# A state-space convolution with a gated feed-forward block: one set of tables for both channel halves, ungated loads, halved last tiles and a new task list

## The chip, the cores and the metric

One core of one Trainium2 chip runs the whole program. The metric is the device time of one execution in microseconds. A core has five engines with queues of their own: PE (TensorE, the matmuls), DVE (VectorE), ACT (ScalarE), POOL (GpSimd) and SP (SyncE, which here only issues DMAs); ACT also issues some DMAs. Sixteen DMA engines serve all of these queues.

## The reference, cut to what matters

```python
def _A_ref(u, A_re, A_im, B_re, B_im, C_re, C_im, log_dt, Dskip):   # u: (1, 2048, 512)
    dt = exp(log_dt)[:, None]
    logdA = dt * (A_re + 1j * A_im)                                  # (512, 128)
    K = einsum("dn,dnl,dn->dl", Cc, exp(logdA[:, :, None] * l), dt * Bc).real
    y = irfft(rfft(pad(u)) * rfft(pad(K)))[:L]                       # causal convolution, length 2048
    return y + u * Dskip

def _B_ref(x, w_gate, w_up, w_down):                                 # 512 -> 1792 -> 512
    return (silu(x @ w_gate) * (x @ w_up)) @ w_down

x = A_u
xn = layernorm(x)
s = _A_ref(xn, ...)
g = silu(_B_ref(xn, B_w_gate, B_w_up, B_w_down))
return x + s * g
```

Each of the 512 channels is convolved with its own kernel K of length 2048; the feed-forward block works on rows of 512.

## The kernel before, in words

**The work.** The feed-forward block is cut into 56 units (8 blocks of 256 rows, 7 chunks of the 1792 hidden columns). A unit has a gate half and an up half (`half_mm`, L699, 24 matmuls each, because every f16 operand is split into a high and a low part) and two groups of six down matmuls (`down`, L741). The weights are scaled and split first: `w_norm` (L604) sums squares, `norm_sum` (L614, L615) adds them over the partitions with a matmul on a tile of constants called `ones`, `w_scale_gu` (L635, L624, L637) makes the scale, `w_split` (L669, L670, L665 to L667) makes high and low parts. Rows of u are normalized by `ln_group` and `x_norm` (L503 to L531) and transposed (L540, copied by L546). A row tile ends with `z`, a PSUM bank that collects all down matmuls, and a SiLU of it on ACT (L748), called `zg`; ten of the sixteen `zg` tiles go out to DRAM (`zg_d`) and come back.

The convolution is a Fourier transform in two stages. `x_stage1` (L563) transforms u and stores it in `ax_d`; `kg_tables`, `kg_trig`, `kg_prod`, `kg_mm` (L1145) and `kg_s1` (L1178) build K and store its first stage in `ak_d`, channel half c = 0 ahead of c = 1. Stage two works on 8 groups n of frequencies for each channel half: `s2_load` loads `ak_d`, `ax_d` and a table `gj` of 320 KB; `s2_mm` and `s2_prod` (L1230, L1237) transform and multiply; `s2_inv` (L1277) transforms back two groups together and stores to `bs_d`, with SP issuing the stores (L1289). `final` loads `bs_d`, u again (L1309) and, for early rows, `zg_d`; does the last inverse matmuls (L1324), multiplies by `zg` on DVE (L1333), adds u on POOL (L1336) or for the last rows on DVE (L1338), and stores from ACT's queue (L1340). There are 14 tiles of two row tiles by half the channels, and the two last row tiles alone with all channels.

**The order.** All of this is a list of tasks. Each `add` names an engine, a duration and the buffers and keys that it reads and writes. A long string, `LIST`, gives the order in which tasks are written out; the queue of each engine runs in that order and waits by semaphores. A small model (`Plan.run`) runs through the same list to choose PSUM banks and places in an arena of 118 KB per partition, within `ROOM`, and `keep_warm` puts filler matmuls on `ones` (L1423) where the model sees PE idle. The model's numbers thus change banks, places and fillers, and nothing of what an instruction takes on the chip. DMAs of one queue are issued in order: one that waits holds those behind it.

**Gates.** In `s2_load` the three loads wait for everything stored under the keys `ax` and `ak0` or `ak1`. In `final` the loads of u and of `zg_d` carry `ready`, the key of all `bs_d` stores of the channel half, as the load of `bs_d` itself does.

Of the kernel before, what the change touches and what calls it, by code (L numbers as in the profile page):

```python
# [13 lines left out]
I32 = mybir.dt.int32  # L14
AF = mybir.ActivationFunctionType
ALU = mybir.AluOpType
# [31 lines left out]
    "#)#(#'#K#&#%#J#L#.#T#i#M#N#k###l#/#O#U#R#j#m#V#n#1#v#P#2#Q#S#D#Y#4#W#-#X#Z#5#+#w#o#x#y#q#,#p#r#*&+#8#z(*#s#t&.(+"  # L48
    "#]&/(,(.#}$&#7#[$'$(${(/$)#C#d#;#{#^&0#|$#(0#e(4#_#`&E#f%S&3$*#g&,#a$+#h#b#c(-#:$$(1$-#<&5$w&v(5$2&:&8$x(6$z$y$,"
    "#>$1$3$|$.(7&=#9%#$/(:(;$4$}#=&;#A(@&x$5$6$<%%%.$7&4$=$>(L$8(<%&(M&A$?$@$k$H$G$I(F(2#@(N$;%$(3&9#?$C&1&u#B$9(=&F"  # L50
    "%/(>%((H$D%2$J#0$K(?#6#3(G(I$:$A$S$R$T$N(O$L$B$t(A(R(S(B(J(K$E&6$F$O$](T$M(X(Z$q(P#E&J(C&@$%&?$Q(8(9(Q$0&y$P#u$U"
    "%)&B(_%T(a(D$V&>(U&C&k%+$^$_&}(V(W$Y(Y([$W%'%7(e(g(`$e(b$X%0$Z$[$b(](c&7(E(d(}$`%*(^)$(f(h(i$h$a$f$c%8%<(w$n$i$l"
    "%9$d$m(x(j(y(k$u(m%-%B%,%A%5(z)#({$j%C$r%P$o$s#$#I(l(n(q%D%:(r%Q%R(o)((|$g)=%6)>)?)))0)F%E$p%=$v)G%>%3%F%?(p)H&D"
    "&I&a)%%G%H&G&L%I%;&H(s&V&K%J&M%L)1)2%M)3):%K%@%4-F%1)I&N&O&Q&P)R)S&W)&)J%N&b-G-K);(t&<)<-L&T)T&2)U)'(u&X#G-M&l(v"
    "&c%O&Y%W&m)])^&w'#&R-H&n&p&o&[-I&q&d&f&i&e&])_&S-J-N)`&_-O&z&^&Z)b-R)*&`)K&s&t'$)i)j-P%V-Q-S&g&h&j-[-`-]&U-U-V-X"
    "-k)k)l)s)t-l)c)+-x-c-W-Y-T-d)@-^-_)B-b-a-y.5#H)a-e-g&-)d-f)A-t-v.6),-|.#&r-o-q.7-Z-h)--m-n-p.4)4)6-r%U-s).)/)L.8"
    ".9)C.:.;-u.$-i-j.%)5)7-z-{)w-}.&.(.')8)9.<-w)D.B)E.W.C.E.D.F)u.).*.+)N.I)V)M.?.A%Y)O.=.>.@.H)W)P)x%`)Q#F.,.e.J.K"
    ".M)e.G%]..)X.-./.L.N*$.X.Q.S.O.P%Z.R)Y)Z.T%[.0.1)m%a._.`%d.f)y'')n.b.3.U.2)z)f)[)o*%){)g%X%i'1.[.^.l.m)h*&.Y)p.a"
    "*'.o*()v.V**.c.|.Z)q%b.])|)r.i.k.n.p.g.h.}/#/$*..j%^/%%e*1)}/&/'/(*#%j.d.q.r%c.s*2//*3%k*)*:%n%f*/%g%s.t&{*0.v%_"
    "/).u*;*+*B*4*C.w%h.x.y.z.{/*/+%o%p*</,/./-*6*D*E/5%t/6/0%q/1/3*,/7%l*-/2/D*5*F*7/8/:/Q/9/>&|%m%r&)*G/</4*>/;/S%u"  # L60
    "*8/@*9%v*=*?/=';/?/E*L&'*M/F/H'%/G*@%w*H*A/R/j/I/k/l/M*N*P*I*J/J/O/K/L*K/i*O%y/N'&/A/B*Q*T*U*V*]/Z/]*X/T/V/X/Y'("
    "*R/[/m/n')/U'**S/W'</P/^*W/C/o/p'2/_*Y*Z'3'=/q*[*h%x/}'+/r/s/`*^'4'5/t/u*o/v*e'E'F'G/a*f*g*i',/c/d'T/e%z&#'6'/%{"
    "/b/f/h/g/y&$*j'9'7*_/{%|'-*k*l'.0U&%*a01/w/x0#&&%}&*/z'>*`*b'?0$'H'I*p0%02*c*q*d*m0&0>*n0+/|0:0<&(0V*w0(0?0X0W0'"
    "*x0Z+$0)+%0[0-*r030*0,'U050B0D0G0Y0^07040I0@0A0C'V0.+.0]'00806'J'M090;0E+/*s0_'@0F0`'N0H*t0/00':'K0=0J0a'S'Y'A'B"
    "+&+''C'D+0*u*v0b0K*y0L0n0c0d0e0g0h0i0k+1+60f*z1/0j0M'q0l0Q'L0p0O0o'Z'O0P0N1#*{0u0v0m+(0r0t0R0S0w0}100q0s*|+)1$+*"
    "0T0y*}+#++0x1G+21H1)1*'R'P1F1J+31K1L1,1I+7+81%1'0z+,+-+:1+1-+4+51315'W181:+911+;12141&1(0{0|'{1617+I19+>+<1M'Q1Q"
    "+=1T1U1O+?+@+A1N'81.'X'['g1[1W']1;1<1P1=+F+G1R'|'}+B+C1>1B1Z1V'^'_1]1^1S1x+D1X1@1_'r'h's'i1A+P1j+Q+X+Y1b1a+a+b't"
    "+E1?1C(#'`1c1e'j1E1w+J'k1k'a1s1d+L($1f+K+c1`24251Y1g+M1l'u1m1o'b1y+R+T231u2728+N1z+O1|2%2'261n291p1D+S1q+k+d1r'c"
    "'l1t2#2$2&'d1h+Z+U2:'e'o'm2;'p+V2G+W1{1}2>1i'n2<2@2=+]+l+[+^2A1v'f2B2(2C2V+H2D(%+_2H(&((+e2I2J2d2?2E2^'v2)'y('+s"
    "'w+`'x2_'z2L2K2M2W2X2F+g2a+f+h2N2e2|()+t2P2R+m2O2Y2Q+i2Z2[2`2*2b+j4^2S2{+n3h2]+u2+2T2U+{2-3j+v3u2m2o3i2h2j+o3w2c"  # L70
    "2,2f2/2.2g3$3%3&202k2l+p+q2n+w2i3k3l3m2p3v2}3#3'+r3x3y+x3n3r+y2135+z3z+|3{3)3*3+3q3(3p,(2q3|3}3o3s4$4#+}4%3t,#22"
# [12 lines left out]
)
LIST = [DIGITS.index(a) * 90 + DIGITS.index(b) for a, b in zip(LIST[::2], LIST[1::2])]
ROOM = 104.0 * 1024
REUSE = 0.25
APART = 8.0
WARM_FROM, WARM_SPAN, WARM_IDLE, WARM_SHARE, WARM_DUR = 1.5, 3.4, 1.0, 0.8, 0.213
# [31 lines left out]
class Plan:  # L121
# [55 lines left out]
    def run(self):  # L177
        order = [self.tasks[i] for i in LIST]
        free = dict.fromkeys(("PE", "DVE", "ACT", "POOL", "SP"), 0.0)
# [3 lines left out]
        dma_free = port_free = 0.0  # L183
# [140 lines left out]
def dma_us(size, pieces):  # L324
    return max(size / 280e3, pieces * 1.2e-3)
# [67 lines left out]
def kernel(  # L393
# [73 lines left out]
    def load(dst, src, names, size, pieces, pr, rd=(), ahead=None):  # L467
        add("SP", 0.4, lambda: sy.dma_start(dst(), src), up=names, rd=rd, pr=pr, dma=dma_us(size, pieces), root=True, ahead=ahead)
# [84 lines left out]
    def x_stage1(j):  # L553
# [11 lines left out]
        for h in range(2):  # L565
            xa = xas[h]
            add("ACT", 0.6, lambda h=h, xa=xa: S.copy(xa.f32(), pa[h].t), rd=[pa[h]], up=[xa], c=5 if j < 4 else 2, pr=pr)
            add("SP", 0.4, lambda h=h, xa=xa: sy.dma_start(ax_d.rearrange("f r t d -> (f r) t d")[:, 2 * j + h], xa.f32()),
                rd=[xa], up=[key("ax")], c=0, dma=dma_us(262144, 128))
# [159 lines left out]
    def down(b, t, c, hh, pos):  # L729
# [15 lines left out]
        if c == NC - 1:  # L745
            j = 2 * b + t
            zg = zgs[j] = buf(f"zg{j}", 2048, "zg" if b < ZK else None, 2)
            add("ACT", 0.69, lambda: S.activation(zg.f32(), z.t, AF.Silu, scale=zsc[:, 1:2]), rd=[z], wr=[zg], c=1, pr=0)  # L748
            if b < ZK:
                add("SP", 0.4, lambda: sy.dma_start(zg_d[j], zg.f32()), rd=[zg], up=[key(f"zgd{j}")], c=0,  # L750
                    dma=dma_us(262144, 128))
# [4 lines left out]
    def prep(hf):  # L756
# [154 lines left out]
        if hf:  # L911
            off = 0
            for k in ("ft", "bh", "ww", "c"):
                w_ = o[k].size // 4
                add("SP", 0.4, lambda k=k, off=off, w_=w_: sy.dma_start(kp_d[:, off:off + w_], o[k].view(I32)),
# [236 lines left out]
    def kg_s1(i):  # L1152
# [39 lines left out]
        for k in range(2):  # L1192
            add("SP", 0.4, lambda k=k: sy.dma_start(ak_d.rearrange("g r s d -> (g r) s d")[:, k * 32:k * 32 + 32, q * 64:q * 64 + 64],
# [14 lines left out]
    def s2_load(n, c):  # L1208
        pr = s2_due(n, c)
        d = ss[n, c] = {}  # L1210
        for nm, src in (("k", ak_d[4 * n:4 * n + 4].rearrange("q r s d -> (r s) q d")), ("x", a_rows(ax_d, n))):
            b = d[nm] = buf(f"a{nm}{n}{c}", 4096, "a" + nm, int(W["c_a"] + 0.5))
            load(lambda b=b: b.f32().rearrange("p (q d) -> p q d", q=4), src[:, :, c * 256:(c + 1) * 256], [b],
                 524288, 512, pr, rd=[key("ax"), key(f"ak{c}")])
        b = gjs[n, c] = buf(f"gj{n}{c}", 2560, "gj", int(W["c_gj"] + 0.5))
        load(lambda: b.f32(), gj[n], [b], 327680, 128, pr, rd=[key(f"ak{c}")])

    def s2_mm(n, c, nm, dst):
# [3 lines left out]
        def mm():  # L1222
            a = b.f32().rearrange("p (q d) -> p q d", q=4)
            if nm == "k":
                g = gjs[n, c].f32()[:, 384:640].rearrange("p (q z m) -> p q z m", q=4, z=2)
# [7 lines left out]
            g = gjs[n, c].f32()[:, 0:256].rearrange("p (q m) -> p q m", q=4)  # L1233
# [6 lines left out]
        add("PE", 0.9, mm, rd=[b, gjs[n, c]], wr=pt, up=dst, c=2, pr=s2_due(n, c), f32=4)  # L1240
# [21 lines left out]
    def s2_inv(m, c):  # L1262
# [5 lines left out]
        def mm():  # L1268
            for r in range(2):
                for q in range(4):  # L1270
                    for i in range(2):
                        n = 2 * m + i
                        jc = gjs[n, c].f32()[:, 256:384].rearrange("p (a r m) -> p a r m", a=2, r=2)
# [5 lines left out]
        add("PE", 1.335, mm, rd=[ys[2 * m, c], ys[2 * m + 1, c], gjs[2 * m, c], gjs[2 * m + 1, c]], wr=pb, up=bhs, c=2, pr=e, f32=5)  # L1279
        for q in range(4):  # L1280
# [8 lines left out]
            add("SP", 0.4, lambda q=q, b=b: sy.dma_start(bs_d[c, m, q].rearrange("k p d -> p k d"), b.f32().rearrange("p (k d) -> p k d", k=2)),  # L1289
                rd=[b], up=[key(f"bs{c}")], c=0, dma=dma_us(262144, 256))  # L1290

    def final(js, cs, c):
# [15 lines left out]
        for h in range(2):  # L1308
            add("SP", 0.6, lambda h=h: sy.dma_start(vw(fx)[h * 64:(h + 1) * 64], xv[h, :, j0:j0 + nj, cs]), up=[fx], rd=ready, pr=pr,  # L1309
                dma=dma_us(131072, 64 * nj), root=True)  # L1310
        if j0 // 2 < ZK:
            z = buf(f"fz{tag}", 2048, "fz", int(W["c_fz"] + 0.5))
            load(lambda: vw(z), zg_d.rearrange("j p d -> p j d")[:, j0:j0 + nj, cs], [z], 262144, 128 * nj, pr, rd=ready + [key(f"zgd{j}") for j in js])
# [157 lines left out]
```

## Time and profile before

| what | value |
|---|---|
| median of three runs | 613.95 us (611.83 to 614.11) |
| the profiled execution | 610.76 us |
| its span, first to last instruction | 609.0 us |
| granted PE clock, mean | 0.987 |
| PE busy | 581.9 us (96%) |
| DVE, ACT, POOL busy | 432.3, 342.1, 326.2 us |
| moved by DMA | 93.10 MB, mean 153 GB/s |

The profiled execution is 3.2 us below the median of the runs; its span and 1.8 us around it make its own time. Rows of the timeline read: start, duration, engine, line, operation, output and inputs, count; in brackets the idle time of the engine just before and what ended it. SPq and ACTq are the queues that issue DMAs, and their rows last from the first issue to the last. The page's rows in tenths divide the span into 40 slices.

### The profile page before, as it was taken

How to read it: one execution, taken by the hardware profiler on the slowest of the kernel's cores; microseconds unless marked ns; L12 is line 12 of the kernel's file. 1: busy time of each engine (PE TensorE's matmuls, PEld its weight loads, DVE VectorE, ACT ScalarE, POOL GpSimd, SP SyncE). 2: the span in 40 equal slices, each digit the busy share in tenths (PEclk: the TensorE clock that was granted, in tenths of full speed). 3: DMA queues.
4: the chain of work that ended last, by engine and by line, in shares of the span. 5: the costliest groups of instructions: out<-in, count | busy, mean ns of one | idle time of the engine just before them, and what ended most of it. 6: DMA issues, size and time to landing. Idle time of an engine off the chain costs nothing.

```text
span 609.0 us, 18323 instructions
## 1 busy us (share of the span) xinstructions
PE 581.9 (96%) x7625; PEld 411.6 (68%) x7625; DVE 432.3 (71%) x988; ACT 342.1 (56%) x697; POOL 326.2 (54%) x301
## 2 busy tenths in 40 slices
PE   4999999999999999999999999999989999999974
PEld 1678886556888678766787677776657656667531
DVE  3777989665798989888779876878848556673313
ACT  5689856655765468667778687746632423131100
POOL 0145522279974768649997799688023341530131
PEclk9999999999999999999999999999989999999978
DMA  8699621024004041025340123556969889999997
GB/s 261 167 286 321 196 79 48 1 97 155 16 3 95 4 113 37 2 68 169 114 110 15 30 79 138 172 129 172 320 180 275 265 246 270 270 286 255 222 265 184
DMA packets 100594, 93.10 MB, mean 153 GB/s; under 512 B 38496, under 2 KB 83808, under 8 KB 100512
## 3 DMA queue, kind: packets, MB, share of 16 engines
q1 hardware_dynamic: 96000, 87.48, 50.0%
q10 hardware_dynamic: 4512, 4.46, 2.8%
q8 instruction: 60, 0.98, 0.7%
q14 instruction: 22, 0.18, 0.1%
HBM read 59.02 MB, written 32.90 MB: 151 GB/s over the span
## 4 chain that ended last, share of the span: by engine, by line
PE 84%; DMA 9%; DVE 3%; issue 1%; ACT 1%; SPq 0%; ACTq 0%; POOL 0%; DVEq 0%; POOLq 0%
PE p L699 45%; PE p L741 21%; PE p L1145 5%; DMA out_dram<-arena 3%; PE p L1230 3%; PE p L1237 2%; DMA arena<-zg_d 2%; DMA arena<-in_A_u_dram 2%; PE p L1277 2%; PE p L563 2%; PE p L1423 2%; PE p L1178 1%; DMA arena<-bs_d 1%; PE p L540 1%; DMA wd<-in_B_w_gate_dram 1%
## 5 line engine op out<-in xcount | busy, mean ns | idle before, releaser
L699 PE MATMUL p<-arena,wu 128*128 128x256 f16 x1344 | 157.3, 274 | 4.0 <-issue 4.0
L741 PE MATMUL p<-wd,arena 128*128 128x512 f16 x672 | 155.4, 381 | 0.0
L699 PE MATMUL p<-arena,wg 128*128 128x256 f16 x1344 | 155.2, 273 | 0.0
L699 PEld LDWEIGHTS <-wu 128*128 128x128 f16 x1344 | 130.7, 98 | 26.9 <-issue 8.8
L699 PEld LDWEIGHTS <-wg 128*128 128x128 f16 x1344 | 129.7, 98 | 23.0 <-issue 3.7
L741 PEld LDWEIGHTS <-arena 128*128 128x128 f16 x672 | 63.5, 98 | 77.1 <-issue 9.3
L1078 POOL TENSOR_TENSOR arena<-arena 128x1536 f32<-128x1536 f32 x32 | 90.7, 2840 | 18.0 <-DVE arena L854 5.6
L720 ACT ACTIVATE arena<-p,inv 128x512 f32<-128x512 f32 x56 | 38.4, 689 | 65.4 <-PE p L699 57.1
L1070 POOL TENSOR_TENSOR arena<-arena 128x1024 int32<-128x1024 int32 x32 | 62.4, 1955 | 18.5 <-DVE arena L830 7.5
L722 DVE SCALAR_TENSOR_TENSOR p<-p,shc,arena 128x512 f32<-128x512 f32 x56 | 42.2, 754 | 30.1 <-PE p L699 17.8
L724 ACT CAST arena<-p 128x512 f16<-128x512 f32 x56 | 32.5, 589 | 33.8 <-DVE p L722 16.4
L1113 DVE TENSOR_TENSOR arena<-arena,p 128x512 f32<-128x512 f32 x64 | 43.6, 681 | 8.4 <-ACT p L1094 6.4
L1336 POOL TENSOR_TENSOR arena<-arena 128x512 f32<-128x512 f32 x12 | 15.1, 1268 | 57.7 <-DMA arena<-in_A_u_dram 37.9
L725 DVE TENSOR_TENSOR arena<-p,arena 128x512 f16<-128x512 f32 x56 | 37.7, 683 | 11.2 <-ACT arena L724 11.2
L1094 ACT ACTIVATE p<-p,halfpi 128x512 f32<-128x512 f32 x64 | 42.4, 664 | 1.4
L1093 ACT ACTIVATE p<-arena 128x512 f32<-128x512 int32 x64 | 38.9, 610 | 6.4 <-DVE arena L1185 2.2
L1095 ACT ACTIVATE p<-arena 128x512 f32<-128x512 int32 x64 | 37.5, 602 | 8.7 <-DVE arena L1115 4.5
L1259 POOL TENSOR_TENSOR arena<-arena 128x512 f32<-128x512 f32 x16 | 20.3, 1275 | 38.5 <-DVE arena L1255 14.1
L1260 POOL TENSOR_TENSOR arena<-arena 128x512 f32<-128x512 f32 x16 | 20.3, 1272 | 31.3 <-DVE arena L1255 17.8
L1119 DVE SCALAR_TENSOR_TENSOR arena<-arena,p 128x256 f32<-128x256 f32 x64 | 26.5, 414 | 12.6 <-ACT p L1095 8.9
L1145 PEld LDWEIGHTS p<-arena 128*32 128x32 f32 x2048 | 29.7, 110 | 6.6 <-issue 4.2
L1145 PE MATMUL p<-arena 128*32 128x64 f32 x2048 | 33.4, 220 | 0.0
(180 smaller groups left out, 814.0 us busy)
## 6 DMA issues: line engine op xcount, KB each, us to landing
ax_d<-arena SPq DMA_DIRECT2D x32, 256.0 KB, 2.6
ak_d<-arena SPq DMA_DIRECT2D x16, 512.0 KB, 6.5
arena<-ak_d SPq DMA_DIRECT2D x16, 512.0 KB, 5.7
arena<-ax_d SPq DMA_DIRECT2D x16, 512.0 KB, 6.7
bs_d<-arena SPq DMA_DIRECT2D x32, 256.0 KB, 4.8
arena<-in_A_u_dram SPq DMA_DIRECT2D x62, 128.0 KB, 5.0
arena<-in_B_w_down_dram SPq DMA_DIRECT2D x14, 512.0 KB, 6.0
arena<-bs_d SPq DMA_DIRECT2D x14, 512.0 KB, 8.5
```

Of the source, the lines that this page charges most:

```text
L699: T.matmul(pg.t[:, i * 256:(i + 1) * 256].rearrange("p (a t) -> p a t", a=2), w[:, wl, d, i * P:(i + 1) * P], x[:, :, xl, d, :], start=(k ...
L720: add("ACT", 0.69, lambda: S.activation(sg.f32(), pg.t, AF.Silu, scale=inv[:, c, 0:1]), rd=[pg], wr=[sg], c=1, pr=e)
L722: add("DVE", 0.75, lambda: V.scalar_tensor_tensor(pu.t, pu.t, shc[:, c:c + 1], sg.f32(), op0=ALU.mult, op1=ALU.mult), rd=[sg], wr=[pu], c= ...
L725: add("DVE", 0.7, lambda: V.tensor_tensor(hh.view(F16)[:, 512:1024], pu.t, hh.view(F16)[:, 0:512], op=ALU.subtract), rd=[pu], wr=[hh], c=1 ...
L741: T.matmul(z.t, h[:, hl, i * 256 + t * P:i * 256 + (t + 1) * P], w[:, wl, i], start=(c == 0 and i == 0 and k == 0), stop=(c == NC - 1 and ...
L1070: G.tensor_tensor(a, h_[:, :, :, None].to_broadcast([P, 2 * GT, 4, 8]), l_[:, :, None, :].to_broadcast([P, 2 * GT, 4, 8]), op=ALU.add)
L1078: G.tensor_tensor(e, p_[:, :, :, None].to_broadcast([P, 3 * GT, 4, 8]), q_[:, :, None, :].to_broadcast([P, 3 * GT, 4, 8]), op=ALU.mult)
L1093: add("ACT", 0.62, lambda: S.activation(tc_.t, a(), AF.Abs, scale=SIN_SCALE), rd=[an], wr=[tc_], pr=pr)
L1094: add("ACT", 0.7, lambda: S.activation(tc_.t, tc_.t, AF.Sin, bias=halfpi, scale=-1.0), rd=[key("ones")], wr=[tc_], c=4, pr=pr)
L1095: add("ACT", 0.62, lambda: S.activation(ts.t, a(), AF.Sin, scale=SIN_SCALE), rd=[an], wr=[ts], pr=pr + 0.2)
L1113: V.tensor_tensor(o[:, :, 0:64].rearrange("p d (s j) -> p d s j", s=2), e[:, :, 0:64].rearrange("p d (s j) -> p d s j", s=2), t[:, :, None ...
L1145: T.matmul(kt[h * 32:(h + 1) * 32, (r * GD + dd) // 4], o[:, ri, dd + h, 64:96], o[:, ri, dd + h, 0:64], start=(ri == 0), stop=(ri == 1), ...
```

## The change

1. `gj` is loaded once for each of the eight groups, not once for each group and channel half: eight loads of 320 KB fewer. The eight tables stay in the arena from their load to the last use in c = 1. They also lose their gate.
2. In `s2_load` the load of `ak_d` waits for `ak0` or `ak1` alone and the load of `ax_d` for `ax` alone; in `final` the loads of u and `zg_d` lose `ready`.
3. The two last row tiles are finished in column halves: two SiLU of 256 columns, two products, two sums, and four stores of 64 KB where there were two of 128 KB, two from SP and two from ACT.
4. The model's numbers are changed (time of an issue, rate of DMAs, first start, share of fillers, `ROOM` 103 KB for 104), and `LIST` is another one, so the order moves on all engines. The task that sets `ones` is now the first on DVE.

```diff
-ROOM = 104.0 * 1024
+ROOM = 103.0 * 1024
...
-WARM_FROM, WARM_SPAN, WARM_IDLE, WARM_SHARE, WARM_DUR = 1.5, 3.4, 1.0, 0.8, 0.213
+WARM_FROM, WARM_SPAN, WARM_IDLE, WARM_SHARE, WARM_DUR = 1.5, 3.4, 1.0, 0.7, 0.213
...
 LIST = (
-    "#)#(#'#K#&#%#J#L#.#T#i#M#N#k###l#/#O#U#R#j#m#V#n#1#v#P#2#Q#S#D#Y#4#W#-#X#Z#5#+#w#o#x#y#q#,#p#r#*&+#8#z(*#s#t&.(+"
+    "###$#(#'#%#&#K#J#L#)#D#T#.#M#i#k#l#U#V#W#Y#N#P#X#/&0#m#O#R#j#n#o#Z#Q#S#1#2#q(*#4#5#*#v#p#w#r#x&+#y(+(,#s$&(.#t#+"
...
-    return max(size / 280e3, pieces * 1.2e-3)
+    return max(size / 255e3, pieces * 1.3e-3)
...
         if c == NC - 1:
             j = 2 * b + t
+            if b == NB - 1:
+                zgs[j] = [buf(f"zg{j}{q}", 1024) for q in range(2)]
+                for q in range(2):
+                    add("ACT", 0.44, lambda q=q: S.activation(zgs[j][q].f32(), z.t[:, q * HD:(q + 1) * HD], AF.Silu, scale=zsc[:, 1:2]), rd=[z], wr=[zgs[j][q]], c=1, pr=0)
+                return
...
             load(lambda b=b: b.f32().rearrange("p (q d) -> p q d", q=4), src[:, :, c * 256:(c + 1) * 256], [b],
-                 524288, 512, pr, rd=[key("ax"), key(f"ak{c}")])
-        b = gjs[n, c] = buf(f"gj{n}{c}", 2560, "gj", int(W["c_gj"] + 0.5))
-        load(lambda: b.f32(), gj[n], [b], 327680, 128, pr, rd=[key(f"ak{c}")])
+                 524288, 512, pr, rd=[key(f"ak{c}" if nm == "k" else "ax")])
+        if c == 0:
+            g = gjs[n] = buf(f"gj{n}0", 2560, "gj")
+            load(lambda: g.f32(), gj[n], [g], 327680, 128, pr)
...
-            add("SP", 0.6, lambda h=h: sy.dma_start(vw(fx)[h * 64:(h + 1) * 64], xv[h, :, j0:j0 + nj, cs]), up=[fx], rd=ready, pr=pr,
+            add("SP", 0.6, lambda h=h: sy.dma_start(vw(fx)[h * 64:(h + 1) * 64], xv[h, :, j0:j0 + nj, cs]), up=[fx], pr=pr,
...
-            load(lambda: vw(z), zg_d.rearrange("j p d -> p j d")[:, j0:j0 + nj, cs], [z], 262144, 128 * nj, pr, rd=ready + [key(f"zgd{j}") for j in js])
+            load(lambda: vw(z), zg_d.rearrange("j p d -> p j d")[:, j0:j0 + nj, cs], [z], 262144, 128 * nj, pr, rd=[key(f"zgd{j}") for j in js])
...
+        if nj == 1:
+            for q, z in enumerate(zgs[j0]):
+                ot = buf(f"ot{tag}{q}", 1024, "ot")
+                sl = slice(q * HD, (q + 1) * HD)
+                add("DVE", 0.42, lambda ot=ot, z=z, sl=sl: V.tensor_tensor(ot.f32(), py.t[:, sl], z.f32(), op=ALU.mult), rd=[py, z], wr=[ot], c=1, pr=pr)
+                add("DVE", 0.42, lambda ot=ot, sl=sl: V.tensor_tensor(ot.f32(), ot.f32(), fx.f32()[:, sl], op=ALU.add), rd=[fx], wr=[ot], c=1, pr=pr, port=True)
+                for h in range(2):
+                    add(("SP", "ACT")[h], 0.6, lambda h=h, ot=ot, sl=sl: (sy, nc.scalar)[h].dma_start(ov[h, :, j0, sl], ot.f32()[h * 64:(h + 1) * 64]),
+                        rd=[ot], up=[key("out")], c=0, dma=dma_us(65536, 64), pr=pr)
+            return
```

Lines further down move by up to 16: in the changed kernel L1237, L1277, L1289, L1309 and L1324 are L1243, L1283, L1295, L1315 and L1330; stores are L1356 for the pairs of row tiles and L1340 for the two last ones; the SiLU is L753, and L750 for the halves.

What moves is shown at three places. The first is DVE's queue at the start. Before, around the task that sets `ones` (with `halfpi`, another constant); `hsq` is the cast that L615 reads, p_99 the bank that L615 writes:

```order
L517 SCALAR_TENSOR_TENSOR rstd<-rt,rstd 128x2
L614 CAST hsq<-ssq 128x1
L474 MEMSET ones 128x128
L474 MEMSET halfpi 128x1
L531 SCALAR_TENSOR_TENSOR arena<-arena,rstd 128x512
L635 TENSOR_SCALAR ssq<-p_99 128x1
```

In the changed kernel the same queue begins, and then, after the statistics, goes on:

```order
L1482 UNCONDITIONAL_BRANCH
L474 MEMSET ones 128x128
L474 MEMSET halfpi 128x1
L503 BN_STATS st_82<-arena 128x6
L504 BN_AGGR mv<-st_82 128x2
```

```order
L614 CAST hsq<-ssq 128x1
L531 SCALAR_TENSOR_TENSOR arena<-arena,rstd 128x512
L546 COPY arena<-p_100 128x512
L635 TENSOR_SCALAR ssq<-p_99 128x1
L624 TENSOR_SCALAR scw<-ssq 128x1
```

`ones` moved ahead of the first statistic, and one copy of a transposed tile moved ahead of L635.

The second place is the end of PE's queue: before, and then in the changed kernel (p_103 and p_104 are the banks `z` of the last row tile; a row with x4 or x2 stands for that many matmuls of one tile).

```order
L741 MATMUL p_103<-wd,arena 128x512
L741 LDWEIGHTS arena
L741 MATMUL p_103<-wd,arena 128x512
L1324 MATMUL p_99<-arena,j_t 64x512 x2
L1466 UNCONDITIONAL_BRANCH
```

```order
L741 LDWEIGHTS arena
L741 MATMUL p_104<-wd,arena 128x512
L1330 MATMUL p_99<-arena,j_t 64x256 x4
L1330 MATMUL p_102<-arena,j_t 64x256 x4
L1330 MATMUL p_100<-arena,j_t 64x256 x4
L1330 MATMUL p_101<-arena,j_t 64x512 x2
```

Behind the last down matmul stand four tiles of `final` where there was one.

The third place is the end of ACT's queue, with buffer numbers: before, from the last cast of the feed-forward block on,

```order
L724 CAST arena_98<-p2_101 128x512
L1340 DMA out_0_dram<-arena_98 64x2x256 x12
L748 ACTIVATE arena_98<-p5_104,zsc_89 128x512
L1340 DMA out_0_dram<-arena_98 64x2x256 x3
L1340 DMA out_0_dram<-arena_98 64x512 x2
L1340 DMA out_0_dram<-arena_98 64x2x256 x2
L748 ACTIVATE arena_98<-p4_103,zsc_89 128x512
L1340 DMA out_0_dram<-arena_98 64x2x256 x4
L1340 DMA out_0_dram<-arena_98 64x512 x2
```

and in the changed kernel (p7_106 and p5_104 are `z` of the two last row tiles):

```order
L1356 DMA out_0_dram<-arena_98 64x2x256 x5
L750 ACTIVATE arena_98<-p7_106,zsc_89 128x256
L1356 DMA out_0_dram<-arena_98 64x2x256 x4
L750 ACTIVATE arena_98<-p7_106,zsc_89 128x256
L1356 DMA out_0_dram<-arena_98 64x2x256 x3
L1340 DMA out_0_dram<-arena_98 64x256
L750 ACTIVATE arena_98<-p5_104,zsc_89 128x256 x2
L1356 DMA out_0_dram<-arena_98 64x2x256 x6
L1340 DMA out_0_dram<-arena_98 64x256
L1356 DMA out_0_dram<-arena_98 64x2x256 x4
L1340 DMA out_0_dram<-arena_98 64x256 x2
L1356 DMA out_0_dram<-arena_98 64x2x256 x5
```

Behind the last SiLU stand 18 stores where there were 6.

100 lines of the change are left out of this document (50 added, 50 removed).

## The prediction

> **What bounds the kernel now.** I read the page first, then what TensorE (PE) waits for, then the timeline at both ends. The page's 40 slices are 15.2 us each:
>
> ```profile
> PE 581.9 (96%) x7625; PEld 411.6 (68%) x7625; DVE 432.3 (71%) x988; ACT 342.1 (56%) x697; POOL 326.2 (54%) x301
> PE   4999999999999999999999999999989999999974
> PEclk9999999999999999999999999999989999999978
> DMA  8699621024004041025340123556969889999997
> ```
>
> PE is full from slice 2 to slice 38; holes stand only in the first and the last two. From slice 28 on the transfers are full too, so a gain on one could be eaten by the other. Two windows give that traffic a rate (PE, PEld, DVE, ACT and POOL busy, clock, DMA share, GB/s):
>
> ```profile
> 420.00:545.00 125.00, 121.05 (x2147) 81.53 (x2137) 80.43 (x162) 45.59 (x95) 44.73 (x34) 0.99 0.89 263
> 545.00:609.00 64.00, 51.01 (x367) 29.20 (x354) 21.66 (x41) 7.25 (x14) 11.30 (x9) 0.91 0.94 237
> ```
>
> What PE waits for says which of the two is the bound (total, times, longest):
>
> ```profile
> PE p L1423 <- DVE halfpi L474: 9.1, 1, 9.1
> PE p L699 <- issue: 4.0, 2, 2.7
> PE p L1324 <- DMA arena<-bs_d: 3.5, 1, 3.5
> PE p L1324 <- DVE arena L1333: 3.0, 2, 2.2
> PE p L563 <- ACT arena L720: 1.1, 1, 1.1
> ```
>
> That is all: 20.7 us. In the second stage (s2_mm, s2_inv) PE never stands for a table or a spectrum. PE is the bound until the tail, the transfers and the store queue after that. So the time is: when PE gets its first useful matmul, plus a sum of matmuls that the change leaves alone, plus the tail.
>
> **The start.**
>
> ```profile
> 7.58 1.06 ACT L604 ACTIVATE wg<-wd 128x1024 bf16<-128x1024 f32 x1 [0.88 <-DMA wd<-in_B_w_gate_dram]
> 8.76 0.16 DVE L614 CAST hsq<-ssq 128x1 bf16<-128x1 f32 x1
> 8.89 0.17 DVE L474 MEMSET ones<- 128x128 bf16 x1
> 9.11 8.10 PE L1423 MATMUL p<-ones 128*128 128x512 bf16 x27 [9.11 <-DVE halfpi L474]
> 9.37 1.33 ACT L530 ACTIVATE arena<-arena,rstd 128x512 f16<-128x512 f32 x2
> 10.12 0.75 DVE L531 SCALAR_TENSOR_TENSOR arena<-arena,rstd 128x512 f16<-128x512 f32 x1 [1.06 <-ACT arena L530]
> 13.35 3.37 PEld L1423 LDWEIGHTS <-ones 128*128 128x128 bf16 x16 [0.28 <-issue]
> 17.26 0.16 DVE L635 TENSOR_SCALAR ssq<-p 128x1 f32<-128x1 f32 x1 [6.38 <-PE p L615]
> 17.64 1.15 ACT L669 ACTIVATE wg<-wd,scw 128x1024 f16<-128x1024 f32 x1 [3.28 <-DVE scw L624]
> 18.80 1.66 DVE L546 COPY arena<-p 128x512 f16<-128x512 f16 x4 [0.22 <-PE p L540]
> 19.53 1.46 PE L1423 MATMUL p<-ones 128*128 128x512 bf16 x6
> 23.81 0.69 DVE L503 BATCH_NORM_STATS2 st<-arena 128x6 f32<-128x512 f32 x1
> 25.81 0.15 DVE L509 TENSOR_SCALAR va<-mv 128x2 f32<-128x2 f32 x1
> 27.84 1.28 DVE L670 SCALAR_TENSOR_TENSOR wg<-wd,scw,wg 128x1024 f16<-128x1024 f32 x1
> 28.65 2.78 PE L699 MATMUL p<-arena,wg 128*128 128x256 f16 x24
> ```
>
> The filler matmuls on ones are meant to run while PE has nothing; here they are in the way. The sum of squares is ready at 8.92, but its matmul L615 is queued behind 27 fillers that could not begin before ones was set at 9.06; DVE stands 6.38 us at L635, ACT 3.28 us at L669. Afterwards DVE sets ones first of all, so 28 fillers of 0.30 (8.10 / 27) take 8.4 us from about 1 us on and end near 9.4. I follow the new queues with these durations. The first weight load is issued one slot later (64 KB more ahead of it; I allow 0.6 as a guess), L604 of wg 8.2 to 9.25, CAST 9.4, L615 9.6. ACT: L530 twice to 10.65, L604 of wu to 11.7. DVE: L531 to 10.9, one copy (1.66 / 4 = 0.4), L635 at 11.3, scale at 11.6. ACT: L669 of wg 11.75 to 12.9, two L604 to 15.0, L669 of wu to 16.15, two L604 to 18.25, L669 of the next wg to 19.4. DVE goes on with three copies and L531, L670 of wg 14.75 to 16.0, of wu to 17.5, CAST of the third pair at 18.4, two pairs of statistics (4 x 0.43 = 1.74), the Newton chain (25.81 to 27.84 = 2.1), L670 of the second chunk 22.4 to 23.7. PE has then done its first unit by 21.3 and nine fillers by 23.3; the second unit's first half starts there, where it stood at 28.65 with the same useful matmuls behind it. That is 5.3; for hops that I rounded I take **-5.0**, and as ends -3 (another 2 us lost on hops) and -5.3.
>
> One thing in the trace speaks against this. PE has two rates: ten fillers from 9.11 to 13.35 took 0.43 each, the next sixteen 3.37, 0.21 each. With fillers that end at 9.4, the stretch to 16.3 holds only some 5 us of small matmuls; if PE fell back to the slow rate there, the 48 matmuls of the first unit would take twice their 0.116 (2.78 / 24), 5.6 us more, and the gain of the start would be gone. But before has the same mix from 17.3 on, and its fillers at 19.53 still take 0.24 each, so the sum takes nothing for it and I keep it as a rival. The Trainium skill states such a rule in "TensorE: Matmul & The Clock Gate", section "What's actually happening": the clock is halved until some 3.4 us of sustained work, and again after an idle window of that length. The trace agrees on the first half, with 4.24 us at the slow rate; taken strictly, the second half makes the thin stretch harmless only if no whole window of it counts as idle, which no run here shows yet.
>
> **Tables, gates, list.** Eight table loads fall away: 8 x 320 KB = 2.6 MB, at 263 GB/s 10.0 us of transfers. On the path that is 0, because PE never waited there; the ends are 0 and what the tail could use of it, below. In exchange 8 x 2,560 bytes per partition stay until the end of stage two, and the room shrinks by 1 KB; a load that found no room would cost PE up to its landing, nearest row 4.2 (gj, quoted below). I take 0, with +4.2 as the end. The reordered middle has 140 changes of matmul shape where 142 stood: 0, with -4.0 to +4.0 as ends, the "issue" waits gone or doubled. Dropping `ready` lets four of the five late zg loads start ahead of the last bs_d stores; their price is in the bytes of the tail.
>
> **The tail.**
>
> ```profile
> 544.36 1.50 PE L1277 MATMUL p<-arena 32*32 32x256 f32 x64
> 556.01 3.12 SPq L468 DMA_DIRECT2D arena<-bs_d  x5
> 559.97 2.24 PE L1324 MATMUL p<-arena,j_t 128*64 128x256 f32 x16
> 579.53 4.06 PE L741 MATMUL p<-wd,arena 128*128 128x512 f16 x18
> 584.72 12.29 ACTq L1340 DMA_DIRECT2D out_dram<-arena  x12
> 588.13 3.68 PE L1324 MATMUL p<-arena,j_t 128*64 128x512 f32 x12 [3.53 <-DMA arena<-bs_d]
> 591.75 7.58 PE L741 MATMUL p<-wd,arena 128*128 128x512 f16 x30
> 597.05 0.69 ACT L748 ACTIVATE arena<-p,zsc 128x512 f32<-128x512 f32 x1 [23.53 <-DMA arena<-in_A_u_dram]
> 597.13 4.70 ACTq L1340 DMA_DIRECT2D out_dram<-arena  x7
> 601.88 0.69 ACT L748 ACTIVATE arena<-p,zsc 128x512 f32<-128x512 f32 x1 [4.14 <-DMA out_dram<-arena]
> 602.29 3.93 ACTq L1340 DMA_DIRECT2D out_dram<-arena  x6
> out_dram<-arena ACTq DMA_DIRECT2D x30, 128.0 KB, 2.8
> arena<-in_gj_dram SPq DMA_DIRECT2D x12, 320.0 KB, 4.2
> SPq L1309 <- DMA arena<-bs_d: 6.4, 4, 1.9
> ```
>
> The last down matmul ends at 599.33. Afterwards: -5.0 (start); -3.5 (the bs_d wait, since those loads come earlier by the start and by PE's order, below); -0.8 (the shorter DVE wait, 3.0 less 2.2); -0.8 (the thirty after the wait ran 7.58 where 30 x 4.06 / 18 is 6.8); -3.3 because three groups of four L1330 now stand behind the last down matmul (1.12 each, 2.24 / 2). It ends at 585.9. Then comes ACT's queue: two half SiLU, 0.45 each as an estimate (0.69 is the whole), to 586.9, and behind them 18 stores, 0.655 each (3.93 / 6), 11.8: 598.7, and 2.8 to land: **601.5**. Before, 13 stores stood behind the first SiLU and 6 behind the last; four stores moved to SP are already out of the 18. The adds in halves on DVE end some 5 us behind PE, inside these 11.8.
>
> The transfers give a second end. Between the last inverse and the end PE now has one half unit more (2.8) and one L1330 group (1.1), so the last L1277 ends at 545.9 - 5.0 - 3.9 = 537.0 and its loads start 10.2 later, as before (556.01 - 545.86): 547.2. From there to the end I count in the queues 12.3 MB before (8.4 in, 3.9 out) and 11.9 after; before took 53.0 us for it, so after ends at 547.2 + 51.3 = 598.5. The later of the two, 601.5, stands.
>
> **Sum.** 609.0 to 601.5 is -7.5. The profiled execution took 610.76 (span and 1.8 around it), the median of the runs is 613.95; against the median: **606.4 us**.
>
> **Rivals.** (1) The tail gives nothing: the SiLU of the last tiles stays stuck behind stores that wait for adds, as the 23.53 and 4.14 show it now, and 31 of the 32 ACT stores still stand in that queue. Only the start is left: 613.95 - 5.0 = 609.0. (2) The stores behind the SiLU overlap better than one per 0.655, and the transfers set the end: -10.5, 603.5; with the issue waits gone too, 599.5. For it: four of five zg loads leave the tail, and late zg data was part of the 12.29. (3) PE falls to its slow rate in the thin stretch of the start: 606.4 + 5.6 = 612.0. (4) Slower, by SP's queue: reads of u, now free of `ready`, stand between the last bs_d stores. SP is in order, so a read that finds no room holds the stores behind it, and all loads of bs_d wait for the last store. Eight such reads at 1.9 us each (the longest in the last row above: total, times, longest of L1309's waits) are 15 us: bs_d loads from 562, transfers to 613.7, so 618.7. It decides from a delay of 3 us, the gap of 601.5 to 598.5, and ends above before from 10.5. Against it: that row has only four such waits in the whole execution. (5) The early ones do nothing, should DVE start late: then -2.5 of the tail alone remains, 611.4.
>
> **Chances.** Forecast 0.40; (1) 0.25; (2) 0.17; (3) 0.05; (4) 0.08; (5) 0.05. The range from (2) with one issue wait less to (3) and (5) is 600 to 612. A measurement of this kernel can tell about 0.5%, 3.1 us: faster below 610.9. Forecast, (2) and nearly all of (1) lie there, less 0.04 for unknown waits in the middle: faster 0.77; (3), (5) and those: same 0.16; slower 0.07.
>
> **What would show it.** Start: fillers from about 1 us, L635 without a long wait, the second unit's L699 near 23.5. Middle: no wait of PE on DMA, gj loads 8. Tail: last L1277 near 537, last L741 near 586, 18 stores after the last SiLU back to back at 0.65. It is wrong if PE shows a new wait in stage two, if SP's waits for u or for room grow past 3 us ahead of the bs_d stores, or if the last SiLU begins later than 590.

## The result, and the profile after

The changed kernel takes 597.46 us (median of 597.17, 597.46 and 600.29) against 613.95: a ratio of 0.9749, 95% interval 0.9719 to 0.9779. The forecast was 606.4 with a range of 600 to 612, so the direction was right and the gain, 16.5 us, is over twice the 7.5 forecast. The profiled execution took 597.17 with a span of 595.4 (before: 610.76 and 609.0).

The same parts of the page (first line busy time, then 40 slices of 14.9 us):

```profile
PE 578.9 (97%) x7626; PEld 410.6 (69%) x7626; DVE 428.6 (72%) x992; ACT 343.3 (58%) x699; POOL 325.8 (55%) x301
PE   9999999999999999999999999999989999999991
PEclk9999999999999999999999999999999999999996
DMA  8998620042030040124331044466776888999997
```

What PE waits for (total, times, longest):

```profile
PE p L699 <- issue: 1.8, 1, 1.8
PE p L1439 <- DVE halfpi L474: 1.1, 1, 1.1
PE p L1243 <- issue: 0.2, 1, 0.2
```

PE is full up to the 39th slice (in the first with fillers). Of 20.7 us of waits 3.1 are left, and in the tail there is none.

The start, in order of time (start, duration, engine, line, count, idle before):

```profile
1.05 8.41 PE L1439 MATMUL p<-ones 128*128 128x512 bf16 x28 [1.05 <-DVE halfpi L474]
8.87 0.16 DVE L614 CAST hsq<-ssq 128x1 bf16<-128x1 f32 x1 [0.55 <-ACT wg L604]
10.48 0.15 DVE L635 TENSOR_SCALAR ssq<-p 128x1 f32<-128x1 f32 x1
19.80 2.11 PE L1439 MATMUL p<-ones 128*128 128x512 bf16 x9
21.74 2.96 PE L699 MATMUL p<-arena,wg 128*128 128x256 f16 x24
```

The fillers run while PE has nothing else, L635 has lost its 6.38 us of idle time, and the second unit's gate half stands at 21.74 instead of 28.65.

The tail of PE, SP's first load of bs_d there, and ACT (ACTq rows are issues of stores):

```profile
530.15 1.49 PE L1283 MATMUL p<-arena 32*32 32x256 f32 x64
541.67 0.55 SPq L468 DMA_DIRECT2D arena<-bs_d  x1
575.88 2.76 PE L741 MATMUL p<-wd,arena 128*128 128x512 f16 x12
580.32 0.47 ACT L750 ACTIVATE arena<-p,zsc 128x256 f32<-128x256 f32 x1 [4.01 <-DMA out_dram<-arena]
580.69 0.47 ACT L750 ACTIVATE arena<-p,zsc 128x256 f32<-128x256 f32 x1
581.01 3.30 ACTq L1356 DMA_DIRECT2D out_dram<-arena  x5
589.25 3.37 ACTq L1356 DMA_DIRECT2D out_dram<-arena  x5
```

The last inverse ends at 531.6, the last down matmul at 578.6 (before 599.33). Then ACT issues 18 stores from 580.37 to 592.62, 0.68 each, and the last lands 2.8 later.

### The profile page after: what moved, and what is told of

Its sections match the earlier page's. It is cut to its first block, busy times and chain, and to the rows that moved or that the text cites. A ratio compares the mean times of both kernels' runs of the same rounds, so it can differ in the third digit from the quotient of the medians.

```text
span 595.4 us, 18328 instructions
## 1 busy us (share of the span) xinstructions
PE 578.9 (97%) x7626; PEld 410.6 (69%) x7626; DVE 428.6 (72%) x992; ACT 343.3 (58%) x699; POOL 325.8 (55%) x301
## 4 chain that ended last, share of the span: by engine, by line
PE 92%; ACT 3%; issue 1%; DVE 1%; DMA 1%; SPq 0%; POOL 0%; POOLq 0%; ACTq 0%
PE p L699 48%; PE p L741 25%; PE p L1150 5%; PE p L1243 3%; PE p L1236 3%; PE p L1330 3%; PE p L1283 2%; PE p L563 1%; PE p L1183 1%; PE p L540 1%; DMA wd<-in_B_w_gate_dram 1%; ACT wu L604 1%; ACT wg L669 1%; PE p L799 1%; ACT wg L604 0%
## 5 line engine op out<-in xcount | busy, mean ns | idle before, releaser
L699 PE MATMUL p<-arena,wu 128*128 128x256 f16 x1344 | 154.7, 273 | 1.9 <-issue 1.8
L1265 POOL TENSOR_TENSOR arena<-arena 128x512 f32<-128x512 f32 x16 | 20.4, 1275 | 47.6 <-PE p L1236 14.3
L1352 POOL TENSOR_TENSOR arena<-arena 128x512 f32<-128x512 f32 x12 | 15.0, 1268 | 51.5 <-DVE arena L1349 39.5
L1124 DVE SCALAR_TENSOR_TENSOR arena<-arena,p 128x256 f32<-128x256 f32 x64 | 26.4, 413 | 18.7 <-POOL arena L1083 11.8
L1253 ACT COPY arena<-p 128x512 f32<-128x512 f32 x32 | 17.4, 591 | 31.0 <-PE p L1236 30.9
```

What stands on the lines that cost most here:

```text
L699: T.matmul(pg.t[:, i * 256:(i + 1) * 256].rearrange("p (a t) -> p a t", a=2), w[:, wl, d, i * P:(i + 1) * P], x[:, :, xl, d, :], start=(k ...
```

## Experiments

Times are medians. The kernel before had medians of 613.3 to 614.9 on the five chips used, and the interval of a ratio is 2 to 3 us to either side. Kernels of different chips are set side by side all the same; a difference of less than that is not told from 0 by the times alone.

**Ones first, alone.** The kernel before, its list otherwise the same:

```
-LIST = [... "#k", "##", ...]     # "##" is the task that fills ones
+LIST = ["##", ...]
```

> The kernel before, with one task moved: the fill of ones stands first in the list. Theory A (the late fill of ones alone held the start, and the start is worth more than the 5.0 us that was forecast): the second unit's first gate half stands near 22 instead of 28.65, PE's wait on DVE at the start falls from 9.1 to about 1, the span falls by 6 to 8 us, the median to 606 to 608. Theory B (the new list around the start does it, ones alone do little): the gate half after 25, the span falls by at most 4, median 610 or more. Theory C (the start gains, the full transfers of the tail eat it): gate half near 22, the last down matmul 6 us earlier, the end less than 3 us earlier, median 611 or more.

Measured: 606.73, ratio 0.9886 [0.9845, 0.9928], span 604.6. The time is theory A's, though the gate half stands at 24.16, not near 22, and the span falls by 4.4 from the profiled 609.0, not by 6 to 8. PE keeps its other waits:

```profile
PE p L1324 <- DMA arena<-bs_d: 5.1, 3, 3.7
PE p L699 <- issue: 4.8, 3, 3.2
PE p L1324 <- DVE arena L1333: 3.0, 1, 3.0
```

**Ones late, alone.** The changed kernel with that one task behind the first cast of a sum of squares.

> The changed kernel with the fill of ones put back behind the first cast of a sum of squares. Theory A: PE's first matmul near 9, the second unit's first gate half near 28.5 instead of 21.74, median 603 to 606, so 6 to 8 us above the changed kernel's 597.46. Theory B (the new list shelters the start): 2 to 4 us above it. Theory C (a late start is taken back later by a tail that waits for transfers or stores): within 2 us of it.

Measured: 605.35, ratio 0.9864 [0.9821, 0.9907], which is 7.1 above the changed kernel's 598.23 in its repeat below. Theory A; the gate half stands at 29.89. Both ways the fill of ones is worth about 7 us in medians, and nothing downstream takes it back.

**New code in the old order, old code in the new order.** The first keeps the list before (ones first) with tables once, free loads and column halves. The second is the reverse; loads that the old code holds back are moved to the first place where they may start.

> The changed kernel's code (tables once, loads free, last tiles in halves) in the order of the list before, ones first as the one move. Theory A (the searched list makes the tail and the middle, the other parts are worth little without it): as the run with ones first alone, less 0 to 2 us, median 605 to 608, and PE's waits on issue and on bs_d in the tail (4.0 and 3.5 before) still there. Theory B (the other parts are the gain, the list only fits them): median 597 to 600, as the changed kernel.

> The kernel before's code (tables loaded twice, loads held until the last stores, last tiles whole) in the order of the changed kernel's list; the 12 loads that this code does not let start before the last stores of a half stand right behind them, the eight second table loads behind the spectra of their block. Theory A (the list is the gain): median 598 to 602, PE's waits as in the changed kernel, under 4 us in all. Theory B (the list only works with loads that are free and tables that stay): a wait of PE on DMA of 2 us or more in stage two or the tail, median 604 or more.

Measured: 608.79 (ratio 0.9941 [0.9902, 0.998]) and 616.67 (1.0065 [1.0032, 1.0098]). Neither has the gain. But the second was caught up in something else; the group of its fillers (count, busy time, mean ns) says:

```profile
L1423 PE MATMUL p<-ones 128*128 128x512 bf16 x128 | 31.0, 393 | 1.1 <-DVE halfpi L474 1.1
```

The plan puts filler matmuls where it thinks PE will stand, and there it thought so 84 times more than before. So both were run again with fillers in the first 60 us only:

```
         for s, e, at in gaps:
+            if s > 60.0:
+                continue
```

> As the run of the new code in the old list, but fillers only in the first 60 us: 43 where it had 58. Theory A: 15 fillers fewer are 3.2 us, of which a part only covered waits for bs_d: median 605 to 607, so the same as ones first alone (606.73), and the rest of the gain needs the new order. Theory B (fillers were all of that run's loss): 600 or less.

> As the run of the old code in the new list, but filler matmuls stand only in the first 60 us of the plan: 48 in all, where that run had 128 (31.0 us of PE, 84 more than the kernel before). Theory A (the list alone carries the tail; that run was slow only by its own fillers, which PE had to work through though nothing was missing): 616.7 less 80 fillers of 0.21 to 0.24 us, median 598 to 600, and PE's waits on DMA stay under 1 us. Theory B (the loads really come late without the freed gates, and the fillers only stood in that time): PE waits on DMA of 5 us or more in the last 120 us, median 605 or more.

Measured: 604.60 (ratio 0.9861 [0.9821, 0.9901]) and 609.60 (0.994 [0.9914, 0.9966]). The first is near its theory A. The second has the time of its theory B, but PE's waits on DMA are 2.6 us there, not 5. With the old code the fillers fall from 31.0 to 13.0 us of PE, and only 7.1 come back: PE's waits rise from 2.9 to 11.6 us, so most of the rest had stood in the time of real waits. The new code gains 2.1 us in the old order (604.60 against 606.73, intervals that overlap almost wholly: not to be told from 0), the new order alone loses 2.9 (609.60), both together gain 8.5 (598.23). What the new order loses with the old code stands in PE's waits:

```profile
PE p L701 <- issue: 2.2, 1, 2.2
PE p L1326 <- DMA arena<-bs_d: 2.1, 1, 2.1
PE p L1232 <- DVE p L724: 1.5, 1, 1.5
PE p L1232 <- ACT arena L722: 1.0, 1, 1.0
PE p L1232 <- DMA arena<-in_gj_dram: 0.5, 2, 0.3
```

L1232 is s2_mm (1236 in the changed kernel). PE stands at the matmuls of stage two, where the kernel before has no wait.

**The parts undone one by one**, each from the changed kernel, with 45 fillers as it has, and the changed kernel itself:

```
 e9   load(fx), load(z): + rd=ready;   load(spectra): rd=[ax, ak{c}];   load(gj): + rd=[ak0]
 e10  gjs[n] -> gjs[n, c], loaded for c = 0 and c = 1
 e11  last two tiles: one SiLU, product, sum of 512 columns, two stores on ACT
```

> The changed kernel once more, to stand beside the other three on the same chip. All theories: median 597 to 599, 2.2 to 2.8 per cent below the kernel before.

> The changed kernel with its loads held as before: a spectrum waits for the stores of both channel spectra, a table for the first half's, u and zg of the output for the last bs_d store of their half. The 12 loads that cannot stand where the list has them stand right behind those stores; fillers as in the changed kernel, 45. The old code in the new list with few fillers lost 11.4 us to the changed kernel (609.6 against 598.2): by PE's positions some 5 to 7 in stage two (437 to 495 us) and 4 in the tail. Theory T (the doubled tables, in SP's queue between the spectra, made the loss in stage two; the gates made the tail's): 3 to 5 us above the changed kernel, 601 to 603, with a wait of PE on bs_d of 2 us or more and none on tables. Theory G (the gates made it all): 607 to 610.

> The changed kernel with the eight tables loaded again for the second channel half, each right behind its block's second spectra; 45 fillers. Theory T: 5 to 7 us above the changed kernel, 603 to 605, PE waiting on tables or on instructions beside them between 470 and 500 us. Theory G (and the prediction, which took the tables at 0): within 1.5 us of the changed kernel.

> The changed kernel with the last two tiles whole: one SiLU of 512 columns, one product, one sum and two stores on ACT for each, in the same order. 17 or 18 stores stay behind the last SiLU and none goes to SP. All theories: 0 to 2 us above the changed kernel, since ACT's stores still set the end; if halves were what let the tail close, 4 us or more.

Measured: again 598.23 (ratio 0.9757 [0.9723, 0.9791]); gates back 601.29 (0.9781 [0.975, 0.9812]); tables twice 605.12 (0.9851 [0.9817, 0.9884]); tiles whole 598.94 (0.9743 [0.971, 0.9776]). So +3.1, +6.9 and +0.7; together 10.7, where undoing all three at once had cost 11.4. Against tiles whole, which ran on the same chip, gates back and tables twice are +2.4 and +6.2. The intervals of gates and halves overlap that of the repeat: halves are nothing that can be told, and the gates rest on the trace, where PE's wait returns in the tail (the execution shown is the slowest of its six, 602.82):

```profile
PE p L1332 <- DMA arena<-bs_d: 4.3, 3, 1.7
```

**Why tables count.** Three kernels keep one set of tables and issue the eight second loads all the same, for nobody.

```
 e13  g = buf(...); load(g, gj[n])          # c = 1: a buffer in the arena, never read
 e16  load(idle, gj[n])                     # 2,560 bytes beside an arena that is smaller by as much
 e17  load(idle_d[n], gj[n])                # idle_d in HBM
```

> The changed kernel, tables kept for both halves, but the eight second table loads are issued all the same, at the places that the run with tables twice gave them, into buffers that nobody reads. Theory S (2.6 MB more and eight more issues in SP's queue make the loss of tables twice): 603 to 606, as that run. Theory R (there the new tables were needed at once and their buffers held up the next spectra; the traffic is nothing): 598 to 600, as the changed kernel. In between, 601 to 602: both, in equal shares.

> The changed kernel with the eight second table loads issued at the places of the run with idle loads, but all into 2,560 bytes per partition of their own beside the arena, which gives up as much. In the run with idle loads ACT's copy of an inverse stood 3.8 us for the landing of a table load that nobody reads, because the copy's buffer takes its place. Theory P (place: a load holds its piece of the arena until it lands, and what comes into that piece waits): 598 to 600, as the changed kernel (598.2). Theory T (traffic: 2.6 MB and eight issues more where the transfers are full from 470 us on): 602 to 605, as the idle loads (604.1). In between: equal parts.

> The same eight loads at the same places, as copies from HBM to HBM, so that they take transfers and an issue on SP but no place on the chip; the arena is as large and laid out as in the changed kernel. Theory P: 598 to 600. Theory T: 602 to 605.

Measured: 604.13 (ratio 0.9846 [0.9803, 0.9889]), 605.00 (0.985 [0.9805, 0.9896]), 602.91 (0.9826 [0.9782, 0.9869]). Loads that nobody reads cost 5.9, so the size of the loss does not need tables that are read. It does not put out that reading for tables twice itself: there PE stands 4.2 us between 470 and 490, most of it at s2_mm, which reads the new tables, while in e13 and e17 it is full in that window and stands behind it. In e13 the next theory seemed to be visible, ACT waiting for a load that nobody reads because its output takes that load's place:

```profile
ACT arena L1298 <- DMA arena<-in_gj_dram: 3.8, 1, 3.8
```

SP, too, stands 11.6 us in e13 in two waits for such landings, and the repeat of the changed kernel has none. But this theory fell too, for the most part: without any place in the arena the loads still cost 4.7 (e17). In e16 SP itself stood 8.7 us for the landing of one idle load before the next into the same bytes, so its 6.8 is not clean. What is shown: eight loads more that nobody reads cost 4.7 to 5.9 us, as transfers of 2.6 MB and as issues on SP; how these two divide stays open. That tables twice loses its 6.9 in the same way is argued from the like size only. And a copy within HBM is not the same transfer as a load (it lands in 6.3 us in the median, the table loads beside it in 5.1). Windows of the changed kernel's repeat, then of e17 (PE, PEld, DVE, ACT, POOL busy, clock, DMA share, GB/s):

```profile
470.00:490.00 20.00, 20.00 (x407) 13.63 (x405) 11.08 (x21) 7.71 (x16) 7.54 (x6) 1.00 0.89 280
490.00:530.00 40.00, 40.00 (x650) 25.31 (x649) 26.45 (x54) 11.88 (x28) 13.77 (x11) 1.00 0.90 235
```

```profile
470.00:490.00 20.00, 20.00 (x396) 12.42 (x394) 10.50 (x19) 8.33 (x17) 7.53 (x6) 1.00 1.03 338
490.00:530.00 40.00, 37.58 (x628) 23.02 (x627) 23.50 (x46) 9.78 (x22) 13.77 (x11) 1.00 0.93 254
```

The transfers were nearly full already. Eight loads more fill them, and PE stands 2.4 us in the next window, nearly all of it in one wait for a product on DVE (2.1 at 516.72). This execution of e17 was the fastest of its six, 2.5 us of span above the repeat's; where the rest of the median's 4.7 stands, no profile shows.

**The stores at the end.**

```
-    add("ACT", 0.6, ... nc.scalar.dma_start(ov[...], ...))
+    add(("SP", "ACT")[eng], 0.6, ...)            # e7: 7 of the last 18 from SP
```

> The changed kernel with 7 of the 18 stores that stand behind the last SiLU issued by SP instead of ACT. Theory A (the issue of stores on ACT, 0.68 each, sets the end): 11 on either queue from 580.4, last issued near 588, span 590 to 591 instead of 595.4, median 592 to 593. Theory B (the transfers set the end; they are 0.9 busy or more from slice 33 to 39): within 1.5 us of the changed kernel.

> As the split stores, with the five stores that stood ahead of the last SiLUs in ACT's queue put behind them, four of these on SP: 15 stores on SP, 12 on ACT. Theory A (the SiLU of the last tiles stood behind stores that waited for sums, and with it the products of DVE): the last SiLU within 1.5 us of the last down matmul, PE without a wait in the tail, span 589.5 to 591.5, median 591.5 to 593.5. Theory B (transfers or GpSimd's sums set the end): as the split alone, 595 to 596.

> The changed kernel with all output stores in the order in which their sums were ready in the trace of the split stores: the stores of the first column half (ready from 521 to 572 us) ahead of the last SiLUs on ACT, 8 pair stores on SP from its last load on, the last 16 in equal shares on both. Theory A (queue order holds the end back): the last sum near 586.3, the last store issued by 588, span 590 to 591.5, median 591.5 to 593. Theory B (from 575 on the transfers are full, with 146 to 280 GB/s, and set the end): 594.5 to 596, as both splits before.

Measured: 595.61 (ratio 0.9705 [0.9668, 0.9741]), 595.44 (0.9697 [0.9666, 0.9728]), 598.50 (0.9748 [0.971, 0.9786]). The split gains 2.6 on the same chip, half of what the queue alone would give; it beats both kernels. (On the page above the transfers are at 0.8 in slices 32 to 34 and at 0.9 from slice 35, not from 33.) With the SiLUs free of the stores ahead of them the end is no earlier than with the split alone; e12's last SiLUs, and its window from 585 (columns as above):

```profile
578.53 0.84 ACT L751 ACTIVATE arena<-p,zsc 128x256 f32<-128x256 f32 x2 [1.15 <-PE p L742]
```

```profile
585.00:590.00 5.00, 0.00 (x0) 0.00 (x0) 0.00 (x0) 0.00 (x0) 1.26 (x1) 0.64 0.91 281
```

From 585 to 590 the transfers now run at 281 GB/s, where the changed kernel's repeat has 197. That the transfers are now the bound is argued from this window, not shown: from 580 to 585 their share in e12 is 0.72, and ACT issues its last eight stores back to back there too, from 586.27 to 591.78, 0.69 each. No run takes more of them off that queue without moving other stores. With the early stores sooner (e14) SP issues its last load of bs_d at 576.68 instead of 573.77 (e12), and PE waits for it:

```profile
PE p L1333 <- DMA arena<-bs_d: 2.2, 2, 1.8
```

The Trainium skill, "DMA: Bandwidth & Descriptors", section "Issuing engines are not separate DMA queues", says that two issuing engines save only the time of issue, since the transfers share the same engines. The split agrees with the first part: 0.68 each on one queue was worth splitting. That the shared transfers are what ended the gain, no run here shows.

**The kernel before again**, for a second profile.

> The kernel before once more, for a second profile. If its runs differ (609 to 616) by waits that come and go, this profile shows PE's waits on issue, on bs_d or on products of other length than 4.0, 3.5 and 3.0, and a span of 609 to 614; if they differ by the clock, the same waits at another mean clock.

Measured: 615.40, span 613.6, clock 0.989 against 0.987. The waits differ, not the clock:

```profile
PE p L1423 <- DVE halfpi L474: 9.9, 1, 9.9
PE p L1324 <- DMA arena<-bs_d: 5.3, 3, 3.1
PE p L699 <- issue: 4.8, 3, 3.6
```

Here 9.1, 3.5 and 4.0 were the numbers on which the prediction stood: 3.4 us less. All waits of PE together are 25.6 us here and 20.7 there, for spans of 613.6 and 609.0.

## Why the prediction was right in direction and too small

- **The tables, "On the path that is 0, because PE never waited there", and the list, "The reordered middle ... 0".** This is the step that failed: each part was priced by the waits of the old order, and the prices were added up. In the old order the price of the tables may even be right: tables, free loads and halves together are worth 2.1 there. The list alone loses 2.9. Both together gain 8.5 in medians, where the sum has 2.5 for everything behind the start. Of the 6.0 between these, 2.9 is the choice of execution (the last point), and the other 3.1 shows up in the rows of the middle and the tail below: the middle was not 0 but 3.4, of which 2.0 are "issue" waits and 1.4 a half clock behind one of them. In the new order the absent wait was the wrong witness: tables loaded twice cost 6.9, and of the 10.0 us of transfers that the prediction worked out for the eight loads, 4.7 to 5.9 come out at the end even if nobody reads them. The prediction had written that from slice 28 on the transfers are full and a gain could be eaten by them, and did not use it for bytes that go away. Since neither kernel, before or after, has a wait on tables, the two traces alone could not have shown this; only parts undone in the new order do.
- **The list's ends.** -4.0 and +4.0 stood for "issue" waits, which did change (4.0 to 2.0). Its value depends on the code: -2.9 with the old loads, +6.4 (604.60 to 598.23) with the new ones.
- **The start, -5.0.** The mechanism and its order of events were right, each step within 2 us (L635 at 10.48 for 11.3, gate half at 21.74 for 23.3), and the sum was 2 us short: 6.6 (613.3 to 606.73 on one chip) and 7.1 in the two experiments. The allowance of 0.6 for a later first weight load was not needed (L604 at 7.68 for 8.2). PE did not fall to its slow rate in the thin stretch: the fillers at 19.80 take 0.23 each. Rivals (3) and (5) are out. In the trace the term was 1.9 too small (28.65 to 21.74 is 6.9).
- **The tail, -3.5, -0.8, -0.8, -3.3.** The last down matmul came at 578.6 instead of 585.9. Of these 7.3 us, 5.4 were there at the last inverse (531.6 for 537.0). By the rows: 1.9 from the start; 1.1 from the wait at L563, at 34, which the sum left out; 2.0 from the issue waits; and 3.1 of matmuls that ran at half clock before (granted 0.52 and 0.50 in the 3 us behind the two stands), which the sum took to stay as long. Behind the stand of 2.67 at 444 the same 23 matmuls took 4.07 that took 2.67 behind the next one (1.4 more), and behind the bs_d wait the twelve L1324 took 3.68 where twelve L1330 take 1.94 in the changed kernel (1.7 more):

```profile
444.01 4.07 PE L699 MATMUL p<-arena,wu 128*128 128x256 f16 x23 [2.67 <-issue]
488.96 2.67 PE L699 MATMUL p<-arena,wu 128*128 128x256 f16 x23 [1.29 <-issue]
574.01 1.94 PE L1330 MATMUL p<-arena,j_t 128*64 128x512 f32 x12
```

  That makes 8.1, or 0.8 more than the rows have in all, which is not placed. The 2.2 of the DVE wait that the prediction kept stood behind the last down matmul and is gone too. That free loads are a part of this is likely (PE waits 4.3 us for bs_d with the gates back, +3.1 in medians), not clear of noise. Rival (4), reads of u that hold up bs_d stores on SP, did not appear: these reads take 0.6 to 0.7 each, and bs_d loads begin 10.0 us after the last inverse, forecast 10.2.
- **The end.** "18 ACT stores x 0.655 = 11.8", then 2.8: measured 12.25 and 2.8. Right in size; from the last down matmul to the end it is 16.8 for 15.6, 1.2 more, since the first of these stores is issued 1.7 us behind it, not 1.0. The split gained 2.6, near the gap of the prediction's two ends, 598.5 and 601.5; that its second end, the transfers, is what it met is not shown. Rival (1), a tail that gives nothing, is out.
- **The halves**, taken at 0.45 per SiLU and no gain: 0.7 us, not to be told from 0.
- **"Against the median: 606.4".** The sum was made on an execution of the kernel before that lay 3.2 us under its median, and the same 3.2 was added to the kernel after. The second profile of the kernel before is 4.6 us longer by 4.9 us of waits, so such a distance can be waits alone; the changed kernel has lost most of them, and its profiled execution is 0.3 under its median. A third of the miss of 8.9 is this (3.2 less 0.3); the rest is the 7.3 of the tail less the 1.2 of the end.

## What to carry to other kernels

Where transfers are nearly full beside a full engine, price removed bytes at their transfer time as one end of the range, even if no one waits for these bytes today. An order that was searched for a set of loads and buffers has no value apart from them: try each part with the order and without it before calling it free. And look in a second execution for which waits come and go: here the distance of a profile to the median went with those waits.

## What the hardware showed beside that

Some of PE's stands cost more than they last. Behind stands on "issue" of 2.67 us (kernel before) and 3.62 us (its second profile), both near 440 us, the granted clock was about half for 3 us; behind 1.79 us (changed kernel) it stayed full. The windows right behind the stand, in this order:

```profile
444.00:447.00 3.00, 2.99 (x15) 2.11 (x16) 0.00 (x0) 0.00 (x0) 2.33 (x2) 0.52 1.08 360
```

```profile
446.60:449.60 3.00, 2.92 (x15) 2.10 (x16) 0.00 (x0) 0.00 (x0) 1.45 (x2) 0.53 0.89 294
```

```profile
435.20:438.00 2.80, 2.80 (x49) 2.16 (x49) 0.00 (x0) 0.00 (x0) 0.00 (x0) 1.00 0.71 252
```

Fifteen matmuls take 2.99 there, where 15 of 0.116 are 1.74, so the stand of 2.67 costs over 1.2 us more. Length alone does not decide it. In all the traces, the last 3 us of PE's work left out, eight stands of 1.5 to 1.83 us were each followed by 3 us at full clock. Of thirteen between 2.09 and 4.03, nine were followed by 0.50 to 0.67, the shortest of them 2.09 (e5); but four were followed by 1.00, the longest of them 3.03 (new code in the old order) and 3.22 (ones first, alone). The Trainium skill, "TensorE: Matmul & The Clock Gate", section "What's actually happening", has the clock fall after an idle window of some 3.4 us; here stands of 2.1 us could be enough, and one of 3.2 was not.

What PE waits for at these places the traces do show. The page lists `q8 instruction: 60, 0.98 MB`, so 60 packets of 16 KB for the 15,345 instructions of PE's queue in the kernel before, or about 256 for each packet. All the traces together have 44 stands of PE on "issue" of 0.2 us or more. In 42 of them PE has done 11,202 instructions, or a multiple of 256 more or fewer (to within one), whatever the order of the kernel, and goes on 1.1 to 1.6 us after such a packet has ended: 444.01 after 442.51 in the kernel before, 435.19 after 433.87 in the changed one. So PE stands there for its next 256 instructions. Why they come late, no run shows; from 441.3 to 444 in the kernel before the transfers were 0.91 busy.
